# An attention and feed-forward kernel on one core: every queue in the order of a list schedule, one whole pair a block

## The chip, the core and the metric

The kernel runs on one core of a Trainium2 chip. The core has a matrix engine (PE, or TensorE, with its weight loads shown as PEld), three engines for elementwise work (DVE or VectorE, ACT or ScalarE, POOL or GpSimd), a queue that issues transfers (SP), and sixteen DMA engines behind it. Each engine takes its instructions in the order of its own queue; between engines, an instruction waits on semaphores. The metric is the time of one execution in microseconds of device time. Lower is better.

## What is computed

Four batches of 12480 tokens with 128 features go through an induced-attention step with 32 inducing rows, and the result through a feed-forward layer with 2048 hidden values. The weights come as 64-bit numbers.

```python
def mab(q, kv):
    s = scale * (q @ kv.transpose(0, 2, 1))
    s = s - s.max(-1, keepdims=True)
    a = np.exp(s)
    a /= a.sum(-1, keepdims=True) + 1e-09
    return a @ kv
h = mab(I, x)                 # 32 rows over all tokens of the batch
x = mab(x, h)                 # every token over the 32 rows
h = x @ w_in                  # 128 -> 2048
g = np.where(h > 0.0, h, np.exp(np.minimum(h, 0.0)) - 1.0)
return (g @ w_out).astype(np.float32)
```

## The kernel before

**Tiling.** A batch is 25 blocks, 15 of 512 tokens and 10 of 480, in seven groups (`GROUPING`). Hidden values are handled in eight pairs of two chunks of 128 each, so a block has eight pairs and the kernel has 800. Pair number n is (batch x 25 + block) x 8 + pair; `ph_253` is the layer-one result of pair 253.

**A pair.** `ffn_in`: two matmuls into `ph` (three buffers in the accumulation memory, PSUM), then `e = exp(ph - 1)` on ACT. The first product is folded: instead of the token's attention output, the layer takes its 32 attention weights (`stk`, stacked in a high part twice and a low part) against `hw`, the attended rows already multiplied by `w_in`, with a row of ones that adds 1. `ffn_mid`: DVE takes `min(max(ph, 1), e)`, which is the wanted activation plus 1. `ffn_split` makes it ready for layer two in one of three ways, set by `PLAN`:

- "N", whole: POOL subtracts 1 from `e`, and layer two multiplies it in full fp32.
- "P": ACT makes a high part `gh`, POOL subtracts 1 from `e` and then makes the low part `gl = e - gh`.
- "D": ACT makes `gh`, and DVE makes `gl`; the pair keeps its `ph` until then.

`ffn_out` adds the pair into `po`, one bank of PSUM per block: for a split pair six matmuls in a single-pass format (`gh` with the high and the low part of the weight, `gl` with the high part, for two chunks), for a whole pair two matmuls in fp32. `PLAN` is "PDNPDPND": three P, three D and two N a block. After the eighth pair DVE transposes `po` into `o`, and four transfers store it.

**The rest.** For every batch there is a first half: load and transpose the tokens (`load_xT`, line 239), scores against the inducing rows, a maximum per phase (two phases of groups), exponentials, and `gather`, the product with the tokens (`ps_hh`), then the normalised rows `hn`, `hT4`, and `hw`. The second half (`attend_...`) takes the scores of each token against the 32 rows, with a softmax over them whose subtraction, multiplication and low part (`alo`) are on POOL, and places the result in `stk` by transfers. The first half of batch b+1 runs beside the feed-forward work of batch b. The first batch has nothing to run beside: `first_batch` loads the tokens, takes the 64-bit weights apart with integer and float steps on DVE, ACT and POOL (`Weight`), and makes the first block's `stk` on DVE alone (line 526). The loads of `w_out` go into buffers that hold tokens before.

**The order.** PE runs in the order in which the program is written: layer one of pair n, layer two of the pair five behind, and then the middle steps of pair n-1; attention steps are put between by a table of due times in blocks (`attend`, `first_half`). The other engines' queues are ordered by the language's scheduler, but for a few instructions that keep the program's order (the `xT` transposes and the exponentials of the first half). Buffers: five `e`, four `gh`, three `gl`, six `s`.

## Time and profile before

| | us |
|---|---|
| median of three runs | 1728.04 (1726.66 to 1728.49) |
| span of the profiled execution | 1726.8 |
| PE busy | 1655.4 (96%) |
| DVE busy | 1532.5 (89%) |
| ACT busy | 1404.8 (81%) |
| POOL busy | 1347.0 (78%) |

The profile gives no time of the profiled execution other than its span; it lies within the three runs. Busy time of PE is not work at its peak: a matmul's shown duration covers its way through the array, and the next one starts before it ends (a 480-token matmul is shown with 0.38 us, and the next one starts 0.22 us later). So prices of PE work are taken from start to start. The same holds in small for DVE and ACT, whose shown durations overlap by about 0.1 us.

### The profile page before, as it was taken

What the parts mean: (1) busy time and instruction counts of PE and PEld (TensorE: products, weight loads), DVE (VectorE), ACT (ScalarE), POOL (GpSimd) and SP (SyncE); (2) the same over time, 40 slices, a digit from 0 to 9 for tenths busy, and PEclk for the clock granted to TensorE, in tenths of its full rate; (3) what the DMA queues carried; (4) which work ended last, traced back from release to release, by engine and by line L of the source; (5) the groups of instructions that cost most, each with busy time, mean ns of one, the idle gap of its engine ahead of it and who ended that gap; (6) DMA issues with size and microseconds to landing.
All of it is one profiled execution on the core that took longest, in us unless ns stands there. A gap on an engine that the chain in (4) does not pass through costs nothing.

```text
span 1726.8 us, 22653 instructions
## 1 busy us (share of the span) xinstructions
PE 1655.4 (96%) x7446; PEld 1174.4 (68%) x7446; DVE 1532.5 (89%) x1618; ACT 1404.8 (81%) x1643; POOL 1347.0 (78%) x970
## 2 busy tenths in 40 slices
PE   6689999999999999999999999999999999999998
PEld 4356766677676666667776676676777777777776
DVE  6889889989899989898899989889989999989986
ACT  6778888788788878878888788788878888888886
POOL 3877778778787877777778777777868888888886
PEclk9599999999999999999999999999999999999999
DMA  7363233322234333232323423412212211121111
GB/s 253 62 95 54 58 64 59 64 50 61 58 52 74 54 75 60 48 61 45 84 50 54 73 61 50 79 35 36 72 30 48 37 32 27 23 37 31 26 19 21
DMA packets 384757, 98.12 MB, mean 57 GB/s; under 512 B 364864, under 2 KB 370784, under 8 KB 384384
## 3 DMA queue, kind: packets, MB, share of 16 engines
q1 hardware_dynamic: 384640, 96.68, 29.0%
q8 instruction: 59, 0.97, 0.2%
q14 instruction: 58, 0.48, 0.1%
HBM read 48.94 MB, written 25.56 MB: 43 GB/s over the span
## 4 chain that ended last, share of the span: by engine, by line
PE 78%; DVE 9%; ACT 4%; issue 3%; DMA 2%; POOL 2%; SPq 0%; DVEq 0%; ACTq 0%; POOLq 0%
PE po L616 56%; PE ph L558 19%; DVE e L572 2%; ACT e L566 2%; DVE xT L239 2%; DVE gl L584 2%; DVE ph L572 1%; PE ps_hh L367 1%; ACT gh L581 1%; PE ps_t L483 1%; PE ps_s L291 1%; DMA w_raw<-in_moe_w_in_dram 1%; DMA xm<-in_x_dram 1%; DMA xq<-in_x_dram 1%; DVE o L623 1%
## 5 line engine op out<-in xcount | busy, mean ns | idle before, releaser
L566 ACT ACTIVATE e<-ph 128x1024 f32<-128x1024 f32 (+1 forms) x800 | 804.0, 1006 | 235.3 <-PE ph L558 228.3
L589 POOL TENSOR_SCALAR e<-e 128x1024 f32<-128x1024 f32 (+1 forms) x500 | 512.3, 1031 | 307.6 <-ACT gh L581 261.7
L594 POOL TENSOR_TENSOR gl<-e,gh 128x1024 fp32r<-128x1024 f32 (+1 forms) x300 | 704.1, 2347 | 17.6
L572 DVE SCALAR_TENSOR_TENSOR e<-ph,e 128x1024 f32<-128x1024 f32 (+1 forms) x500 | 592.2, 1188 | 78.5 <-ACT e L566 76.4
L558 PE MATMUL ph<-stk,hw 128*128 128x512 f32 (+1 forms) x1600 | 566.0, 435 | 33.1 <-DVE gl L584 14.9
L616 PE MATMUL po<-gh,wo_h 128*128 128x512 f32 (+1 forms) x1200 | 469.1, 391 | 10.5 <-ACT e L566 6.5
L616 PE MATMUL po<-gh,wo_l 128*128 128x512 f32 (+1 forms) x1200 | 465.7, 388 | 0.0
L558 PEld LDWEIGHTS ph<-stk,hw 128*128 128x128 f32 x1600 | 293.5, 190 | 211.4 <-issue 100.6
L572 DVE SCALAR_TENSOR_TENSOR ph<-ph,e 128x1024 f32<-128x1024 f32 (+1 forms) x300 | 359.2, 1197 | 45.2 <-ACT e L566 44.0
L584 DVE SCALAR_TENSOR_TENSOR gl<-ph,gh 128x1024 fp32r<-128x1024 f32 (+1 forms) x300 | 355.9, 1186 | 26.5 <-ACT e L566 10.1
L616 PE MATMUL po<-gl,wo_h 128*128 128x512 f32 (+1 forms) x1200 | 368.5, 388 | 2.4 <-POOL gl L594 2.4
L616 PE MATMUL po<-e,wo_n 128*128 128x512 f32 (+1 forms) x800 | 367.2, 581 | 0.0
L581 ACT ACTIVATE gh<-e 128x1024 fp32r<-128x1024 f32 (+1 forms) x300 | 311.4, 1038 | 21.9 <-DVE e L572 17.8
L581 ACT ACTIVATE gh<-ph 128x1024 fp32r<-128x1024 f32 (+1 forms) x300 | 301.0, 1003 | 10.2 <-DVE ph L572 8.6
L616 PEld LDWEIGHTS po<-gh,wo_h 128*128 128x128 f32 x1200 | 226.0, 188 | 63.3 <-ACT s L300 5.6
L616 PEld LDWEIGHTS po<-gl,wo_h 128*128 128x128 f32 x1200 | 225.8, 188 | 47.7 <-POOL gl L594 3.5
L616 PEld LDWEIGHTS po<-gh,wo_l 128*128 128x128 f32 x1200 | 226.3, 189 | 45.5 <-issue 0.4
L616 PEld LDWEIGHTS po<-e,wo_n 128*128 128x128 f32 x800 | 151.0, 189 | 106.2 <-issue 91.7
L623 DVE STREAM_TRANSPOSE o<-po 128x512 f32<-128x512 f32 (+1 forms) x100 | 69.3, 693 | 12.1 <-PE po L616 12.1
L239 DVE STREAM_TRANSPOSE xT<-xq 128x1024 f32<-128x1024 f32 (+2 forms) x39 | 45.2, 1160 | 0.0
L367 PE MATMUL ps_hh<-xm,e 128*32 128x128 f32 (+2 forms) x872 | 33.3, 295 | 8.2 <-DVE bias L324 2.4
L500 POOL TENSOR_TENSOR s<-s,mx 128x512 f32<-128x512 f32 (+3 forms) x28 | 28.8, 1027 | 14.7 <-DVE mx L499 14.6
(94 smaller groups left out, 575.1 us busy)
## 6 DMA issues: line engine op xcount, KB each, us to landing
xm<-in_x_dram SPq DMA_DIRECT2D x32, 512.0 KB, 4.5
out_dram<-o SPq DMA_DIRECT2D x240, 64.0 KB, 2.0
xq<-in_x_dram SPq DMA_DIRECT2D x84, 128.0 KB, 3.6
out_dram<-o SPq DMA_DIRECT2D x160, 60.0 KB, 1.9
stk<-ahi SPq DMA_DIRECT2D x118, 64.0 KB, 2.0
xq<-in_x_dram SPq DMA_DIRECT2D x60, 120.0 KB, 3.4
stk<-ahi SPq DMA_DIRECT2D x80, 60.0 KB, 2.0
stk<-alo SPq DMA_DIRECT2D x59, 64.0 KB, 2.0
```

The source lines that it names most:

```text
L239: tc.keep_in_program_order(nc.vector.transpose(t, xq.rearrange("p u d -> p (u d)")))
L367: nc.tensor.matmul(ps[c * Q : (c + 1) * Q, :C], st["e", g][:np_, u * Q : (u + 1) * Q], st["xm", g, u - u % UP][:np_, u % UP, :], start=(u ...
L500: eng.tensor_tensor(out=s, in0=s, in1=mx.unsqueeze(2).broadcast_to([np_, U, Q]), op=ALU.subtract)
L558: nc.tensor.matmul(ph[:, i], state[b]["hw"][:, f * P : (f + 1) * P], stacks[b, k], start=True, stop=True,)
L566: nc.scalar.activation(e, ph, AF.Exp, bias=-1.0)
L572: nc.vector.scalar_tensor_tensor(out=v["g"], in0=v["ph"], scalar=1.0, in1=v["e"], op0=ALU.max, op1=ALU.min)
L581: nc.scalar.activation(v["gh"], v["g"], AF.Copy, bias=-1.0)
L584: nc.vector.scalar_tensor_tensor(out=v["gl"], in0=v["g"], scalar=-1.0, in1=v["gh"].bitcast(F32), op0=ALU.add, op1=ALU.subtract,)
L589: nc.gpsimd.tensor_scalar(out=v["e"], in0=v["e"], scalar1=-1.0, scalar2=1.0, op0=ALU.add, op1=ALU.mult)
L594: nc.gpsimd.tensor_sub(v["gl"], v["e"], v["gh"].bitcast(F32))
L616: nc.tensor.matmul(po[:, :T], w, g, start=(cp == 0 and i == 0), stop=(cp == NCP - 1 and i == len(parts) - 1),)
L623: nc.vector.transpose(o.rearrange("p u d -> p (u d)"), po[:, :T])
```

## The change

**A list schedule.** The kernel no longer writes its instructions down as it goes. Each one is recorded as an `Op` with its engine, a key (where it is wanted, in pairs), a length and a delay worked out by small formulas, and what it reads and writes. `Program.order()` then goes through all of them, with buffers, PSUM banks and transfers kept account of: at each step it takes, over the engines, the ready instruction that can start first (for ACT and DVE the one of smallest key among those that could start within 60 ns). The instructions are issued in the order of the starts so found, and `manual_schedule()` without a list of engines keeps that order on every queue, SP's included.

**The plan** is "PDPDPDPN": four P, three D, one N.

**Layer two** is recorded in two pieces for a split pair (`gh` and `gl`); the first piece issued for a block starts the sum, the last one ends it, whichever they are.

**The first batch** runs its maxima in five phases of groups instead of two, so that first gathers do not wait for later groups; the weights are taken apart in slices of 512 instead of 256, with the sign put in by integer operations on DVE (one ACT and one POOL instruction less a slice); `hn` is made on ACT.

**Buffers**: `gl` has two for P and two for D pairs, `s` five instead of six. The step that adds 1e-9 to a row sum (line 511) is a two-input form with a tile of zeros.

```diff
-PLAN = "PDNPDPND"
+PLAN = "PDPDPDPN"
+KMID, KGL, KOUT = 1.0, 1.6, 5.0
+KGH = {"D": 1.5, "P": 2.0}
+BUF = dict(e=5, gh=4, glD=2, glP=2)
+LOOKS = {"PE": 0.0, "ACT": 60.0, "DVE": 60.0, "POOL": 0.0, "SP": 0.0}
...
+    def order(self):
...
+        while len(done) < len(self.ops):
+            best = None
+            for e, row in there.items():
...
+                for op in row:
+                    if op.at is not None and op.at <= base + self.LOOK[e]:
+                        if cand is None or (op.key, op.n) < (cand.key, cand.n):
+                            cand = op
+                if best is None or cand.at < best.at:
+                    best = cand
...
+        return sorted(done, key=lambda o: (o.start, o.n))
+
+def act(n, psum=False):
+    return 0.828 * n + (54 if psum else 69), 118.0
...
+        add("DVE", key + 4.0, dve(n, True)[0], lambda: nc.vector.transpose(
+            t(), xq().rearrange("p u d -> p (u d)")
+        ), r=[(xq, dq) for dq in range(4)], w=[(t, 0)], lag=108)
...
+        add("DVE", n + KMID, dve(2 * T)[0], lambda: nc.vector.scalar_tensor_tensor(
+            out=ga(), in0=ph()[:, :, :T], scalar=1.0, in1=e(), op0=ALU.max, op1=ALU.min
+        ), r=[(ph, 0), (e, 0)], w=[(g, 0)], lag=108)
...
+        pieces = [[v for v in parts if v[0] < 2], [v for v in parts if v[0] == 2]]
+        for m, piece in enumerate(pieces):
...
+            def layer_two(piece=piece):
+                for _, w, g_ in piece:
+                    nc.tensor.matmul(
+                        po()[:, :T], w(), g_(), start=po.count == 0, stop=po.count == po.total - 1
+                    )
+                    po.count += 1
...
-        nc.vector.tensor_scalar_add(sm, sm, EPS)
+        add("DVE", later, 62.0, lambda: nc.vector.scalar_tensor_tensor(
+            out=sm()[:np_], in0=sm()[:np_], scalar=EPS, in1=none[:np_, :U],
+            op0=ALU.add, op1=ALU.add,
+        ), r=[(sm, 0)], w=[(sm, 0)], lag=108)
...
-    PHASES = [range(0, 3), range(3, NG)]
+    PHASES0 = [range(0, 2), range(2, 4), range(4, 5), range(5, 6), range(6, 7)]
+    PHASES = [range(0, 3), range(3, NG)]
...
-    ctx.enter_context(tc.issue_after(last.ins))
-    ET = mybir.EngineType
-    ctx.enter_context(tc.manual_schedule(engines={ET.PE}))
+    todo = prog.order()
+    ctx.enter_context(tc.manual_schedule())
+    for op in todo:
+        op.fn()
```

**Three places where the order changes.** The first is PE in the seventh block of batch one. `ph` is layer one, `po` layer two; the first number after `ph`, `gh`, `gl` or `e` is that of the pair. Before:

```order
L558 MATMUL ph_254_5545<-stk1_135,hw_1_4194 128x512 x2
L616 MATMUL po_1_6_5533<-gh_249_5473,wo_h_127 128x512
L616 MATMUL po_1_6_5533<-gh_249_5473,wo_l_128 128x512
L616 MATMUL po_1_6_5533<-gh_249_5473,wo_h_127 128x512
L616 MATMUL po_1_6_5533<-gh_249_5473,wo_l_128 128x512
L616 MATMUL po_1_6_5533<-gl_249_5475,wo_h_127 128x512 x2
L558 MATMUL ph_255_5562<-stk1_135,hw_1_4194 128x512 x2
L616 MATMUL po_1_6_5533<-e_250_5464,wo_n_126 128x512 x2
L558 MATMUL ph_256_5571<-stk2_137,hw_1_4194 128x512 x2
```

The same place of the changed kernel:

```order
L736 MATMUL ph_254_5879<-stk1_177,hw_1_498 128x512 x2
L736 MATMUL ph_255_5882<-stk1_177,hw_1_498 128x512 x2
L796 MATMUL po_1_6_5826<-gl_250_5870,wo_h_174 128x512 x2
L796 MATMUL po_1_6_5826<-gl_251_5868,wo_h_174 128x512 x2
L796 MATMUL po_1_6_5826<-gh_252_5872,wo_h_174 128x512
L796 MATMUL po_1_6_5826<-gh_252_5872,wo_l_175 128x512
L796 MATMUL po_1_6_5826<-gh_252_5872,wo_h_174 128x512
L796 MATMUL po_1_6_5826<-gh_252_5872,wo_l_175 128x512
L796 MATMUL po_1_6_5826<-gh_253_5885,wo_h_174 128x512
L796 MATMUL po_1_6_5826<-gh_253_5885,wo_l_175 128x512
L796 MATMUL po_1_6_5826<-gh_253_5885,wo_h_174 128x512
L796 MATMUL po_1_6_5826<-gh_253_5885,wo_l_175 128x512
```

Before, every layer one was followed by the whole of the pair five behind. Now two layer ones stand in a row (in this block 251 and 253 are D pairs, 250, 252 and 254 are P, 255 is the N pair), `gh` and `gl` pieces of different pairs follow, and layer two is two to four pairs behind.

The second is POOL beside it. `L589` and `L765` subtract 1 from `e`; `L594` and `L769` make `gl`; the row with `s2` is a step of the attention's softmax. Before:

```order
L589 TENSOR_SCALAR e_248_5413<-e_248_5413 128x1024
L594 TENSOR_TENSOR gl_248_5441<-e_248_5413,gh_248_5438 128x1024
L589 TENSOR_SCALAR e_250_5464<-e_250_5464 128x1024
L589 TENSOR_SCALAR e_251_5480<-e_251_5480 128x1024
L594 TENSOR_TENSOR gl_251_5526<-e_251_5480,gh_251_5523 128x1024
L589 TENSOR_SCALAR e_253_5531<-e_253_5531 128x1024
L589 TENSOR_SCALAR e_254_5548<-e_254_5548 128x1024
L594 TENSOR_TENSOR gl_253_5560<-e_253_5531,gh_253_5557 128x1024
```

Now:

```order
L765 TENSOR_SCALAR e_248_5784<-e_248_5784 128x1024
L769 TENSOR_TENSOR gl_248_5833<-e_248_5784,gh_248_5810 128x1024
L765 TENSOR_SCALAR e_250_5804<-e_250_5804 128x1024
L769 TENSOR_TENSOR gl_250_5870<-e_250_5804,gh_250_5831 128x1024
L765 TENSOR_SCALAR e_252_5847<-e_252_5847 128x1024
L769 TENSOR_TENSOR gl_252_5899<-e_252_5847,gh_252_5872 128x1024
L765 TENSOR_SCALAR e_254_5895<-e_254_5895 128x1024
L765 TENSOR_SCALAR e_255_5905<-e_255_5905 128x1024
L769 TENSOR_TENSOR gl_254_5947<-e_254_5895,gh_254_5916 128x1024
```

Four subtractions in eight pairs stand where three stood, each right behind the step that it needs.

The third is PE in the first batch, before any feed-forward work: `ps_x` transposes tokens, `ps_s` are scores of a group (the number behind it), `ps_pm` is part of a maximum, `ps_hh` gathers a group. Before:

```order
L291 MATMUL ps_s_4_381<-xT_8_358,indT 32x480 x2
L291 MATMUL ps_s_4_381<-xT_9_359,indT 32x480 x2
L291 MATMUL ps_s_5_423<-xT_10_400,indT 32x480 x2
L259 MATMUL ps_x_8_453<-ident,xm_6_8_177 128x64 x7
L291 MATMUL ps_s_5_423<-xT_11_401,indT 32x480 x2
L291 MATMUL ps_s_6_462<-xT_12_442,indT 32x480 x2
L367 MATMUL ps_hh_0_482<-xm_0_0_151,e_0_480 32x128 x8
```

Now:

```order
L477 MATMUL ps_pm_0_344<-apart_0_329,nsel_160 128x8
L866 MATMUL ps_x_0_348<-ident,xm_3_0_213 128x96 x8
L451 MATMUL ps_s_2_360<-xT_4_340,indT 32x512 x2
L451 MATMUL ps_s_2_360<-xT_5_342,indT 32x512 x2
L523 MATMUL ps_hh_0_374<-xm_0_0_197,eT_0_366 32x128 x8
L523 MATMUL ps_hh_0_374<-xm_0_8_201,eT_0_366 32x128 x8
L523 MATMUL ps_hh_1_396<-xm_1_0_205,eT_1_372 32x128 x8
L523 MATMUL ps_hh_1_396<-xm_1_8_207,eT_1_372 32x128 x8
L866 MATMUL ps_x_8_430<-ident,xm_3_8_218 128x96 x8
```

The first gather, behind which the buffers of two token pieces come free for the loads of `w_out`, stood behind the scores of all seven groups and now stands behind those of three.

More of the change, by code (lines that the diff above doesn't have):

```diff
@@ L219 @@
-    xT = {}
-    state = {}
-    steady = []
-    def in_order(ins):
-        return tc.keep_in_program_order(ins) if steady else ins
-    def load_xT(b, h):
+    ind = const.tile([M, C], F32, name="ind")
+    indT = const.tile([C, M], F32, name="indT")
+    win_sb = const.tile([C, F], F32, name="win_sb")
+    wo_n = const.tile([P, max(1, len(CHUNKS_N)), C], F32, name="wo_n")
+    wo_h = const.tile([P, NSPLIT, C], F32R, name="wo_h")
+    wo_l = const.tile([P, NSPLIT, C], F32R, name="wo_l")
+    homes = [const.tile([P, TM], F32R, name=f"stk{i}") for i in range(STK)]
@@ new lines, in block_xT, with parts_xT, start @@
+    def block_xT(b, k):
+        h, j = HALF_OF[k]
+        T = BLOCKS[k][1]
+        return xT[b, h]()[:, j * T : (j + 1) * T]
+    def parts_xT(b, k):
+        h, _ = HALF_OF[k]
+        U = BLOCKS[k][1] // Q
+        return [(xT[b, h], v) for v in range(0, 1 if b else U, UP)]
+    def start(b, key):
+        st = get(b)
+        st["pm"] = new([P, NG], F32, "pm", f"pm_{b}")
+        st["es"] = new([P, NG], F32, "es", f"es_{b}")
+        add("POOL", key, 60.0, lambda: nc.gpsimd.memset(st["pm"](), -3.0e38),
+            w=[(st["pm"], g) for g in range(NG)], lag=45)
+        add("POOL", key, 60.0, lambda: nc.gpsimd.memset(st["es"](), 0.0),
+            w=[(st["es"], g) for g in range(NG)], lag=45)
@@ new lines @@
+    for i, groups in enumerate(PHASES0):
+        for g in groups:
+            transpose_first(g)
+            scores(0, g, CH + g)
+        bias_of(0, i, groups.stop, CH + groups.stop - 1)
+        for g in groups:
+            weights_of(0, g, i, CH + g)
+            gather(0, g, CH + g, g == 0, get(0)["scale", i] if i and g == groups.start else None)
+    sum_es(0, PHASES0, CH + 7)
+    share_of(0, CH + 7)
+    norm_h(0, CH + 7)
+    spread_h(0, CH + 7)
+    attend(0, 0, CH + 8, 0.0, lone=True)
@@ new lines, with piece @@
+    project_h(0, CH + 8)
+    for quarter in range(4):
+        n = NFC // 4
+        raw = new([P, n, 2 * C], U32, "xm" if quarter < 2 else "e", f"w_out_{quarter}")
+        rows = w_out[quarter * n * P : (quarter + 1) * n * P, :]
+        load_raw(raw, lambda raw=raw, rows=rows: nc.sync.dma_start(
+            raw(), rows.rearrange("(c p) d -> p c d", p=P)), LOADS[3] + 0.01 * quarter)
+        prog.writer[("w_out",)] = prog.ops[-1]
+        key = KWOUT + quarter * KWSTEP
+        done = (raw, 0, "lo")
+        weight_steps(raw, 0, key, lambda raw=raw: words_of(raw, 0)[0].bitcast(F32), [done])
+        for j in range(n):
+            f = quarter * n + j
+            def piece(raw=raw, j=j):
+                return words_of(raw, 0)[0].bitcast(F32)[:, j * C : (j + 1) * C]
+            if f in WHERE_N:
+                add("ACT", key + 0.1 * j, act(C)[0], lambda f=f, piece=piece: nc.scalar.copy(
+                    wo_n[:, WHERE_N[f], :], piece()), r=[done], w=[("wo", f)], lag=118)
@@ L641, in first_half, with key @@
+                add("POOL", key + 0.1 * j, pool_two(C)[0] + 100,
+                    lambda w=w, piece=piece: nc.gpsimd.tensor_sub(
+                        wo_l[:, w, :], piece(), wo_h[:, w, :].bitcast(F32)
+                    ), r=[done, ("woh", f)], w=[("wo", f)], lag=50)
     def first_half(b):
-        steps = [(0.0, lambda: start(b))]
+        base = (b - 1) * NBLK
+        def key(at):
+            return (base + at) * NCP
+        start(b, key(0.0))
         at = 0.0
+        first = 0.0
@@ L665, in first_half @@
+                gather(b, g, key(at + 1.19), g == 0,
+                       get(b)["scale", i] if i and g == PHASES[i].start else None)
                 at += gap
[L666 to L672 removed]
```

1193 lines of the change are left out of this document (646 added, 547 removed).

## The prediction

> **What bounds the kernel now.** I read the page's first part, then the busy time in four stretches of the same phase of the work, then the chain of waits inside a stretch, then single rows.
>
> ```profile
> span 1726.8 us, 22653 instructions
> PE 1655.4 (96%) x7446; PEld 1174.4 (68%) x7446; DVE 1532.5 (89%) x1618; ACT 1404.8 (81%) x1643; POOL 1347.0 (78%) x970
> ```
>
> The span stands 1.2 us under the median of the runs (1728.04); the sum is made against the span and the forecast is given as it comes out. The page shows nothing around the span that would add to it.
>
> ```profile
> core 0: us, PE busy (x) PEld busy (x) DVE busy (x) ACT busy (x) POOL busy (x), PEclk, DMA share, GB/s
> 89.13:507.79 418.66, 406.52 (x1825) 287.26 (x1826) 375.77 (x386) 341.37 (x386) 324.78 (x223) 1.00 0.33 61
> 507.79:926.47 418.68, 408.64 (x1836) 287.50 (x1835) 377.15 (x389) 342.94 (x388) 326.37 (x223) 1.00 0.32 60
> ...
> 1344.82:1726.80 381.98, 376.72 (x1514) 277.10 (x1513) 336.79 (x328) 317.36 (x351) 313.53 (x214) 1.00 0.16 28
> ```
>
> Each stretch is one batch of 25 blocks (the cuts are at the same layer-two pair of each batch's first block; the third of the four, left out, ends 418.4 us after its start, at 1344.82). PE is busy for 408.6 of 418.7 us and idle for 10; in the last batch, where no next batch's first attention half runs beside it, it is idle for 5.3 us of 382.0, and that lies at the end:
>
> ```profile
> by line: PE po L616 74.2%; PE ph L558 23.0%; PE ps_t L483 1.5%; DVE o L623 0.2%; issue 0.0%
> ...
> 1721.58 0.68 DVE L623 STREAM_TRANSPOSE o<-po 128x480 f32<-128x480 f32 x1 [3.91 <-PE po L616]
> ```
>
> The first row is the chain of waits in the last batch: nothing but matmuls. PE's work is the bound there to the last 5 us, which are the transpose from 1721.58 and the store behind it. In batch one the chain holds other things:
>
> ```profile
> by line: PE po L616 54.3%; PE ph L558 18.5%; issue 3.6%; DVE e L572 3.3%; DVE xT L239 2.9%; DVE gl L584 2.7%; ACT e L566 2.7%; ACT gh L581 1.8%; PE ps_hh L367 1.7%; DVE ph L572 1.5%; PE ps_s L291 1.4%; DMA xq<-in_x_dram 1.4%; PE ps_t L483 1
> ...
> 533.36 3.40 DMA xq<-in_x_dram
> 563.63 2.31 DMA xq<-in_x_dram
> ```
>
> These are places where DVE's queue stood at a transpose whose load had not landed, and PE then lacked a `ph` buffer. So PE's work sets the pace, and order costs some 10 us a batch.
>
> **The whole pair that becomes a split one.** PE first. A whole (N) pair is four passes of fp32 matmul, a split pair six single ones:
>
> ```profile
> 1353.72 1.72 PE po L616 x4
> ...
> 1662.43 1.61 PE po L616 x4
> 1664.48 1.31 PE po L616 x6
> ```
> ```profile
> 1355.73 0.39 PE L616 MATMUL po<-gh,wo_h 128*128 128x512 f32 x1
> ...
> 1357.11 0.63 PE L558 MATMUL ph<-stk,hw 128*128 128x512 f32 x2
> ```
>
> The first fence is the chain (1.72 us for an N pair of 512 tokens, 1.61 at 480, a split pair 1.31 at 480); in the second, a split pair of 512 lasts from 1355.73 to 1357.11, 1.38. A batch has 15 blocks of 512 and 10 of 480, so PE loses 15 x 0.34 + 10 x 0.30 = **8.1 us a batch**: 408.6 becomes 400.5, and the last batch's 376.7 becomes 368.6.
>
> ACT gains one `gh` a block, POOL one subtraction (the pair's `-1` on POOL stays, since an N pair had it too):
>
> ```profile
> L594 POOL TENSOR_TENSOR gl<-e,gh 128x1024 fp32r<-128x1024 f32 (+1 forms) x76 | 178.4, 2347 | 4.7
> L581 ACT ACTIVATE gh<-e 128x1024 fp32r<-128x1024 f32 (+1 forms) x76 | 78.9, 1038 | 6.0 <-DVE e L572 4.7 <-PE ps_t L483 0.4 <-PE ps_hh L367 0.4
> ...
> L531 POOL TENSOR_TENSOR alo<-aT,ahi 128x512 fp32r<-128x512 f32 (+3 forms) x7 | 8.8, 1258 | 0.0
> L513 POOL TENSOR_TENSOR s<-s,sm 128x512 f32<-128x512 f32 (+3 forms) x7 | 7.3, 1036 | 0.0
> L500 POOL TENSOR_TENSOR s<-s,mx 128x512 f32<-128x512 f32 (+3 forms) x7 | 7.2, 1027 | 3.7 <-DVE mx L499 3.7
> L511 DVE TENSOR_SCALAR sm<-sm 128x16 f32<-128x16 f32 (+3 forms) x7 | 2.9, 420 | 0.0
> ```
>
> These groups are of batch one. ACT: 342.9 + 25 x 1.04 = 369 us a batch. DVE keeps 377, less about 2 for the EPS step of line 511, which becomes another form; both stay under PE's 400. POOL is the question, and its busy time alone misleads, since a subtraction waits for the `-1` just ahead of it:
>
> ```profile
> 1430.49 1.06 POOL L589 TENSOR_SCALAR e<-e 128x1024 f32<-128x1024 f32 x1 [1.41 <-ACT gh L581]
> 1431.63 2.39 POOL L594 TENSOR_TENSOR gl<-e,gh 128x1024 fp32r<-128x1024 f32 x1
> 1433.97 1.07 POOL L589 TENSOR_SCALAR e<-e 128x1024 f32<-128x1024 f32 x1
> ...
> 1704.45 1.00 POOL L589 TENSOR_SCALAR e<-e 128x960 f32<-128x960 f32 x1 [1.30 <-ACT gh L581]
> 1705.53 2.24 POOL L594 TENSOR_TENSOR gl<-e,gh 128x960 fp32r<-128x960 f32 x1
> 1707.74 0.99 POOL L589 TENSOR_SCALAR e<-e 128x960 f32<-128x960 f32 x1
> ```
>
> From start to start a P pair holds POOL for 1.14 + 2.34 = 3.48 us at 512 and 1.08 + 2.21 = 3.29 at 480. With four of them and one lone `-1` (1.0) a block takes 14.9 and 14.1: 15 x 14.9 + 10 x 14.1 = 365 a batch, and with the attention's three groups (23) and one memset of about 1.8 it is **POOL 389 us a batch against PE's 400**, 97%. In the last batch three of the groups' first steps lie ahead of it in the new order, so POOL has 380 and PE 368.6. There POOL becomes the bound: 380 + 5.2 for the end is 385 against 382.0 now, **+3 us**. Bounds: 374 if POOL's lead hides it all (-8), 397 if POOL stands idle for 3% (+15).
>
> A rule speaks against the added subtraction. The Trainium skill, "GPSIMD Engine Reference", section 4.1 "Engine selection", says to put elementwise work on the Vector engine, where two-input operations take about half the time. The row of line 594 (2347 ns) beside DVE's `gl` below (1186 ns) agrees with the factor. By that rule the new pair would be of kind D, and DVE would carry 25 x 1.1 = 28 us more a batch, 405 in all, past PE's 400: here POOL is the place with room, and the sum is left as it is.
>
> ```profile
> L584 DVE SCALAR_TENSOR_TENSOR gl<-ph,gh 128x1024 fp32r<-128x1024 f32 (+1 forms) x76 | 90.2, 1186 | 8.3 <-ACT e L566 3.4 <-PE po L616 3.2 <-ACT gh L581 0.8
> ```
>
> **The order.** In the new one the `xT` transposes stand four pairs (some 7 us) behind their loads, so the two DMA waits above go; the scores, gathers and `alo` are spread between pairs; layer one comes as two pairs in a row with both D and P parts summed when they are there. What is late next: a `ph` buffer of a D pair, freed only by its second DVE step, and `gl`, with two buffers for P and two for D instead of three for all. Walking pairs 248 to 257 in the new order (a part of it stands above), PE has about 8 us of work between `ph_253` and `ph_256`, and the D pair's path (exp 1.0, DVE 1.2, `gh` 1.0, DVE 1.2, hand-overs) about 5: it fits, with 3 us for what else ACT and DVE hold. Summing in any order is worth little by itself, as PE's wait for POOL's `gl` is 5.9 us in the whole run (3.5 for the weight load, 2.4 for the matmul). I bound PE's idle time per batch by 0 (its middle of the last batch, with the others at 82 to 88%) and by 25 (two and a half times today's 10, for POOL at 97%) and take **6**, between the row of the last batch and today's, since the waits on loads go and POOL's come. A batch is then 400.5 + 6 = 406.5 against 418.6: **-12 us, three times -36** (bounds -54 and +21).
>
> **The start.**
>
> ```profile
> 32.95 3.04 SPq L200 DMA_DIRECT2D w_raw<-in_moe_w_out_dram  x4
> 52.71 0.86 DVE L409 TENSOR_SCALAR hn<-h,r 128x128 f32<-128x128 f32 x1
> 67.00 1.11 DVE L526 TENSOR_TENSOR stk<-aT_-1_804,stk 32x512 fp32r<-32x512 f32 x1
> 68.16 1.22 PE L558 MATMUL ph<-stk,hw 128*128 128x512 f32 x2 [9.36 <-DVE stk L526]
> 77.94 0.88 POOL L214 TENSOR_TENSOR wo_l<-wo,wo_h 128x128 fp32r<-128x128 f32 x2
> 83.92 1.88 PE L616 MATMUL po<-e,wo_n 128*128 128x512 f32 x4
> ...
> 40.00:60.00 20.00, 12.64 (x136) 7.63 (x136) 15.50 (x36) 14.65 (x41) 14.75 (x25) 0.50 0.58 95
> 70.00:85.00 15.00, 11.99 (x33) 7.76 (x28) 12.31 (x14) 11.69 (x17) 13.51 (x14) 0.66 0.00 0
> ```
>
> The loads of `w_out` wait for a buffer until the first gather is done, at 32.95; the first layer one starts at 68.16, and the weights are being finished until 78. In the new order the first two gathers stand ahead of groups 3 to 6, so `w_out` can be asked for about 8 us sooner; its words stand ahead of the last groups on DVE and ACT, so `hn` gains 5 or 6 us and not 8; from `hn` to layer one (14.6 us now, with 4 us of weight steps in between) 1 us goes. First layer one at about 61, **-7**. From 68.16 to the N pair at 83.92 pass 15.8 us with 7 us of full-speed PE work in them; with all weights done before, I take another **-6**. Together **-13**, bounds -5 (the weights only change places) and -20. PE runs at half clock there (0.50 and 0.66 granted in the last two rows), which stays.
>
> **Sum.** 1726.8 - 13 - 36 + 3 = 1681.
>
> **Rivals.** *The order takes nearly every wait*: PE idle 1 a batch, batches of 401.5 (-51), start -20, end +3: 1659. For it: the last batch runs without any. Against: POOL at 97% where it was 78%. *Most is given back*: idle 15 a batch (415.5, -9 in all), start -10, end +6: 1714. For it: ACT, DVE and POOL all stand above 90% of PE's time, in queues that keep their order. *POOL sets the pace, slower than before*: POOL's work is 3 x 389 + 380 = 1547, and what lies around the four batches in the forecast is 1681 - 3 x 406.5 - 385 = 76. Before each of its 400 subtractions POOL has to see `gh` of ACT and a `gl` buffer read by PE.
>
> ```profile
> POOL e L589 <- ACT gh L581: 261.7, 217, 4.4
> ```
>
> Such waits are 1.2 us each today and cost nothing while POOL has room. Where they cost over (1727 - 76 - 1547) / 400 = 0.26 us a subtraction, the kernel is slower; at 0.3 us it takes 1743. Against: a look-ahead of several pairs in the rows, and `gh` stands two or more rows ahead on ACT. *POOL's subtraction stretches as DVE gets denser*: at 5% (a size I choose, since no row shows one) it is 400 x 0.12 = 47 us on POOL, so 401 a batch, level with PE, and 392 in the last: 12 us more there make 1693. The trace shows none of it: 2347 ns in batch one, and the row below in the last.
>
> ```profile
> L594 POOL TENSOR_TENSOR gl<-e,gh 128x1024 fp32r<-128x1024 f32 (+1 forms) x74 | 173.9, 2350 | 3.8
> ```
>
> The Trainium skill, "GPSIMD Engine Reference", section 1 "Specifications", names this one: the memory ports are shared with the Vector engine, in contention when its instruction has two SBUF inputs. Here nearly all of DVE's steps read one side from PSUM.
>
> **How the numbers follow.** Forecast 1681: 0.45. Nearly no wait, 1659: 0.20. Given back, 1714: 0.18. Stretched, 1693: 0.04. POOL's pace, 1743: 0.13. The forecast's own range is 1665 to 1698. The range of 1650 to 1726 leaves out the slower case and the tip of the fastest, under 2 in 10. 0.2% of the time is 3.5 us, about what a measurement of this kernel can tell from none. Slower by more: 0.13; within: 0.04, the upper end of the given-back case; faster: 0.83.
>
> **What would show it.** Right: PE busy near 400 in a full batch and idle under 10; POOL busy near 385; in the last batch PE waiting for POOL's `gl`, and that line in the chain; first layer one near 61. Wrong: POOL idle between pairs for `gh` while PE waits for `gl` (the slower case); PE idle above 15 with `ph` waiting for DVE (given back); a first layer one at 66 or later; a subtraction above 2.45 us.

## The result, and the profile after

The changed kernel takes **1746.47 us** (median of 4 runs, 1744.96 to 1747.35) against 1727.94 of the kernel before beside it: ratio **1.0109, 95% interval 1.0094 to 1.0123**. It is slower, and outside the range of 1650 to 1726 that was given.

The first two lines of the page after stand beside those of before: PE 12 us more, ACT 83 and POOL 217 more.

```profile
span 1744.0 us, 23334 instructions
...
PE 1667.7 (96%) x7652; PEld 1198.6 (69%) x7652; DVE 1530.7 (88%) x1610; ACT 1487.9 (85%) x1710; POOL 1564.5 (90%) x1041
```

To compare stretches, the prediction's cut (the first block's whole pair) no longer serves: that pair was the third of eight and is now the last. The cut used from here on is the start of DVE's transpose of `po`, the end of a block, for the first block of each batch and for the last block of all. Both views are of busy time in stretches: from, to, length, then each engine's busy time and number of instructions, and behind POOL the granted clock. First the kernel before:

```profile
0.00:101.89 101.89, 66.48 (x481) 42.28 (x482) 75.27 (x137) 68.94 (x142) 64.90 (x96) 0.78 0.57 149
101.89:523.10 421.21, 410.53 (x1847) 290.11 (x1847) 381.04 (x394) 344.67 (x391) 329.63 (x227) 1.00 0.32 60
523.10:941.77 418.67, 408.63 (x1836) 287.48 (x1835) 377.17 (x389) 342.99 (x388) 326.37 (x223) 1.00 0.32 60
941.77:1358.19 416.42, 406.43 (x1827) 286.19 (x1826) 374.41 (x386) 341.71 (x387) 322.88 (x221) 1.00 0.28 52
1358.19:1721.58 363.39, 363.35 (x1461) 268.38 (x1459) 323.87 (x316) 306.44 (x339) 303.23 (x206) 1.00 0.17 29
```

The changed kernel:

```profile
0.00:119.18 119.18, 74.37 (x506) 44.78 (x506) 81.82 (x139) 61.46 (x109) 57.17 (x69) 0.76 0.58 147
119.18:533.94 414.76, 408.54 (x1904) 294.66 (x1904) 377.79 (x395) 366.72 (x417) 385.63 (x252) 1.00 0.29 61
533.94:953.14 419.20, 409.70 (x1884) 293.33 (x1884) 380.55 (x395) 365.46 (x415) 383.84 (x249) 1.00 0.31 62
953.14:1364.04 410.90, 404.88 (x1863) 294.56 (x1864) 367.36 (x379) 361.69 (x410) 381.19 (x247) 1.00 0.22 47
1364.04:1738.90 374.86, 370.24 (x1497) 271.25 (x1495) 322.47 (x308) 332.56 (x363) 356.64 (x228) 1.00 0.14 26
```

So of the 17.2 us between the two spans, the start has **+17.3**, the three batches **-11.4** (-6.5, +0.5, -5.5), the last stretch **+11.5**, and the end behind it -0.1. The forecast for the same three terms was -13, -36 and +3 (at cuts some 13 us earlier). The four stretches behind the start sum to the same as before, and what the kernel loses is the start.

The chain of waits of the last stretch, by line, was all matmuls before (quoted in the prediction). After, an eighth of it is POOL:

```profile
by line: PE po L796 50.7%; PE ph L736 16.9%; POOL gl L769 7.3%; ACT e L746 4.3%; issue 4.1%; POOL e L765 4.0%; ACT gh L755 3.2%; DVE gl L760 2.2%; DVE e L750 1.8%; DVE ph L750 0.9%; POOL alo L705 0.8%; DMA stk<-ahi 0.7%; POOLq L1012 0.6%; D
```

The start, rows of the timeline by engine (start, length; in brackets the idle time before and what ended it):

```profile
23.72 2.39 SPq L901 DMA_DIRECT2D w_out<-in_moe_w_out_dram  x4
...
27.97 0.77 DVE L364 TENSOR_SCALAR w_part<-w_in 128x512 uint32<-128x512 uint32 x2 [2.62 <-DMA w_in<-in_moe_w_in_dram]
31.77 0.69 DVE L378 SCALAR_TENSOR_TENSOR w_part<-w_in,w_part 128x512 uint32<-128x512 uint32 x1 [2.83 <-POOL w_part L374]
35.45 1.28 DVE L875 COPY xT<-ps_x 128x512 f32<-128x512 f32 x2
...
36.19 1.93 PE L451 MATMUL ps_s<-xT,indT 128*32 128x512 f32 x6 [8.18 <-DVE xT L875]
83.45 2.92 PE L736 MATMUL ph<-stk,hw 128*128 128x512 f32 x6
```

DVE waits for the load of `w_in` and then for POOL at its weight slices, with copies of tokens queued behind them until 35.45; PE stands 8.18 us for one of these copies, and the first layer one comes at 83.45 instead of 68.16. The delay is there before the attended rows are normalised: the step `hn` starts at 68.62, where before it started at 52.71. The loads of `w_out` are asked for 9 us sooner, as foreseen.

### The profile page after: what moved, and what is told of

It is laid out like the page before. It is cut to its first block, busy times and chain, and to the rows that moved or that the text cites. A ratio compares the mean times of both kernels' runs of the same rounds, so it can differ in the third digit from the quotient of the medians.

```text
span 1744.0 us, 23334 instructions
## 1 busy us (share of the span) xinstructions
PE 1667.7 (96%) x7652; PEld 1198.6 (69%) x7652; DVE 1530.7 (88%) x1610; ACT 1487.9 (85%) x1710; POOL 1564.5 (90%) x1041
## 4 chain that ended last, share of the span: by engine, by line
PE 63%; POOL 13%; DVE 11%; issue 6%; ACT 5%; DMA 2%; SPq 0%; POOLq 0%; DVEq 0%; ACTq 0%
PE po L796 45%; PE ph L736 15%; POOL gl L769 7%; POOL e L765 4%; DVE e L750 3%; ACT e L746 2%; DVE gl L760 2%; DVE ph L750 2%; ACT gh L755 2%; PE ps_t_False L645 1%; PE ps_s L451 1%; POOL alo L705 1%; PE ps_hh L523 1%; DVE apart L471 1%; DVE sm_False L679 1%
## 5 line engine op out<-in xcount | busy, mean ns | idle before, releaser
L769 POOL TENSOR_TENSOR gl<-e,gh 128x1024 fp32r<-128x1024 f32 (+1 forms) x400 | 940.0, 2351 | 19.5
L765 POOL TENSOR_SCALAR e<-e 128x1024 f32<-128x1024 f32 (+1 forms) x500 | 511.9, 1031 | 100.2 <-ACT gh L755 87.0
L796 PE MATMUL po<-gh,wo_h 128*128 128x512 f32 (+1 forms) x1400 | 557.1, 398 | 3.7 <-DVE o L807 2.0
L796 PE MATMUL po<-gh,wo_l 128*128 128x512 f32 (+1 forms) x1400 | 546.1, 390 | 0.0
L736 PE MATMUL ph<-stk,hw 128*128 128x512 f32 (+1 forms) x1600 | 488.9, 405 | 25.2 <-DVE e L750 16.3
L755 ACT ACTIVATE gh<-e 128x1024 fp32r<-128x1024 f32 (+1 forms) x400 | 417.9, 1045 | 39.1 <-DVE e L750 35.9
L796 PE MATMUL po<-gl,wo_h 128*128 128x512 f32 (+1 forms) x1400 | 444.0, 410 | 5.9 <-POOL gl L769 5.6
L796 PEld LDWEIGHTS po<-gl,wo_h 128*128 128x128 f32 x1400 | 253.4, 188 | 118.4 <-POOL gl L769 55.3
L796 PEld LDWEIGHTS po<-gh,wo_h 128*128 128x128 f32 x1400 | 263.7, 188 | 85.8 <-ACT gh L755 14.7
L796 PEld LDWEIGHTS po<-gh,wo_l 128*128 128x128 f32 x1400 | 263.6, 188 | 54.1 <-issue 3.3
L796 PE MATMUL po<-e,wo_n 128*128 128x512 f32 (+1 forms) x400 | 187.5, 591 | 0.5 <-POOL e L765 0.5
L796 PEld LDWEIGHTS po<-e,wo_n 128*128 128x128 f32 x400 | 75.7, 192 | 58.6 <-issue 48.6
L807 DVE STREAM_TRANSPOSE o<-po 128x512 f32<-128x512 f32 (+1 forms) x100 | 69.2, 692 | 11.5 <-PE po L796 11.2
L451 PE MATMUL ps_s<-xT,indT 128*32 128x512 f32 (+1 forms) x200 | 33.0, 642 | 16.8 <-DVE xT L875 10.7
```

The lines of the kernel that those rows point to most:

```text
L451: nc.tensor.matmul(ps()[j * Q : (j + 1) * Q, :T], indT, block_xT(b, g0 + j), start=True, stop=True)
L736: nc.tensor.matmul(ph()[:, j, :T], st["hw"]()[:, f * P : (f + 1) * P], homes[i][:, :T], start=True, stop=True,)
L755: add("ACT", n + KGH[how], act(2 * T, how == "D")[0], lambda: nc.scalar.activation(gh(), ga(), AF.Copy, bias=-1.0), r=[(g, 0)], w=[(gh, 0) ...
L765: add("POOL", n + KMID, pool_one(2 * T)[0], lambda: nc.gpsimd.tensor_scalar(out=e(), in0=e(), scalar1=-1.0, scalar2=1.0, op0=ALU.add, op1= ...
L769: add("POOL", n + KMID, pool_two(2 * T)[0], lambda: nc.gpsimd.tensor_sub(gl(), e(), gh().bitcast(F32)), r=[(e, 0), (gh, 0)], w=[(gl, 0)], ...
L796: nc.tensor.matmul(po()[:, :T], w(), g_(), start=po.count == 0, stop=po.count == po.total - 1)
```

## The experiments

All twelve runs, cut as above (us; the last column is the measured ratio to the kernel before with its interval):

| | to the first block's end | batch | batch | batch | last | median | ratio |
|---|---|---|---|---|---|---|---|
| before | 101.9 | 421.2 | 418.7 | 416.4 | 363.4 | 1728 | |
| after | 119.2 | 414.8 | 419.2 | 410.9 | 374.9 | 1746.5 | 1.0109 [1.0094, 1.0123] |
| e1 after, WARM 0 | 104.7 | 414.6 | 419.2 | 410.9 | 374.8 | 1735.4 | 1.0035 [1.0024, 1.0047] |
| e2 after, old plan | 119.7 | 420.4 | 419.9 | 411.6 | 378.9 | 1758.4 | 1.0174 [1.0159, 1.0189] |
| e3 before, new plan | 98.5 | 426.6 | 423.2 | 421.8 | 372.2 | 1750.0 | 1.0127 [1.0110, 1.0144] |
| e4 after, one piece | 121.2 | 426.1 | 424.1 | 418.9 | 377.5 | 1774.2 | 1.0266 [1.0251, 1.0281] |
| e5 after, light POOL | 117.1 | 409.1 | 408.5 | 400.8 | 365.5 | 1708.1 | 0.9892 [0.9875, 0.9908] |
| e6 after, no tiny steps | 119.1 | 411.4 | 410.9 | 407.1 | 376.0 | 1731.0 | 1.0016 [1.0007, 1.0025] |
| e7 e1 + true durations | 103.8 | 412.7 | 415.8 | 411.9 | 379.4 | 1730.6 | 1.0016 [1.0007, 1.0025] |
| e8 e3, light POOL | 101.3 | 418.1 | 416.5 | 415.5 | 366.8 | 1725.3 | 0.9986 [0.9976, 0.9995] |
| e9 e1 + e6 | 103.6 | 411.4 | 410.6 | 407.3 | 375.8 | 1714.7 | 0.9924 [0.9912, 0.9937] |
| e10 before, no tiny steps | 101.5 | 421.3 | 417.8 | 415.4 | 364.1 | 1727.1 | 0.9998 [0.9989, 1.0006] |
| e11 e9, later hand-over | 102.6 | 412.7 | 411.1 | 407.8 | 368.5 | 1711.3 | 0.9905 [0.9890, 0.9920] |
| e12 e11, old plan | 104.9 | 411.7 | 408.2 | 405.4 | 379.9 | 1717.0 | 0.9936 [0.9920, 0.9953] |

**e1: the schedule's PE lengths at the start.** The schedule counts every PE length twice before `WARM` (in `order()`: `if op.eng == "PE" and start < self.warm: hold *= 2`).

```diff
-WARM = 40000.0
+WARM = 0.0
```

> The changed kernel, but its schedule is made as if PE ran at full clock from the start (WARM 0 instead of 40000 ns). Theory start-order (the schedule held PE's steps at double length before 40 us, where the trace grants full clock, so token copies and gathers were queued on DVE and ACT behind weight steps): the first layer one moves from 83 us to 68 to 74, the total falls by 9 to 16 us against the changed kernel (1746), to about 1733. Rival start-work (five phases and weights done early are simply more work ahead of the first layer one): first layer one stays at 80 or later, total within 4 us of 1746.

1735.4 us, 11 less than the changed kernel by the medians and 14.7 less by the spans of the profiled executions (1729.3 and 1744.0); that of e1 is the fastest of its six, and where the others lose up to 5 us is not shown. The cut shows where: the first block ends at 104.7 instead of 119.2 (-14.5), and nothing else moves by more than 0.2. In its trace `hn` starts at 51.84 and the first layer one comes at 71.86:

```profile
71.86 2.50 PE L736 MATMUL ph<-stk,hw 128*128 128x512 f32 x5
```

For the doubling there is no ground in the trace: in the first 40 us the granted clock was 0.99 before, and 0.90 even in the changed kernel with its stalls. With PE thought slow, the schedule set DVE's weight slices ahead of the token copies for which PE then stood; in e1 the first slice of `w_in` starts on DVE at 30.13, behind most of these copies.

**e2 and e3: the plan and the order apart.** e2 is the changed kernel with the old plan, e3 the kernel before with the new one.

```diff
-PLAN = "PDPDPDPN"
+PLAN = "PDNPDPND"
```

> The changed kernel with the plan of before (two whole pairs a block). Theory POOL-bound: the last batch, 383 us of which POOL was busy 360 and PE waited for its low parts, falls to 380 at the same cut less about 8, the three other batches come to 410 to 413 from 415 on the mean, the total falls to 1722 to 1732, with the start as late as in the changed kernel. Rival list-order: the order itself costs PE its time, so that with PE's work up by 8 us a batch the batches take 420 or more and the total is 1755 or more.

> The kernel before, with the plan of the changed one and nothing else. Theory POOL-bound: start as before (first layer one at 68), the last batch 390 to 395 (10 above before) and the three others within 6 us of before, total 1725 to 1740. Rival list-order (POOL is no bound, the new order spoils it): batches 8 us shorter each and the last one as well, total near 1697.

Neither part pays alone. e2 lands in the range of its second theory, 1755 or more. e3 lies above both: its batches and its last stretch are as its first theory had them, its total is 10 us over. The new plan in the old order costs 22 us, though it takes PE work away: the batches are 4.5 to 5.4 longer, the last stretch 8.8. In that run PE waits for DVE's `gl` ahead of layer one. The D pairs, three a block as before, now stand at every second place, and each keeps its `ph`; that this is the reason was not tried alone:

```profile
PEld ph L558 <- DVE gl L584: 87.5, 88, 2.2
...
PE ph L558 <- DVE gl L584: 37.4, 48, 1.8
```

(us in all, times, longest; the same two rows before are 24.8 and 14.9.) The old plan in the new order speaks against the view that POOL's load alone makes the changed kernel slow: with POOL at 325 to 328 a batch two of the three batches stay where they were before (the third is 4.8 shorter), and the last stretch is 15.5 longer. With about the same load on POOL as before, PE's weight loads wait for its `gl` ten times as long (the first row is of the kernel before, the second of e2), so the new order alone sets layer two close behind POOL:

```profile
PEld po L616 <- POOL gl L594: 3.5, 3, 2.8
```
```profile
PEld po L796 <- POOL gl L769: 37.0, 89, 0.9
```

**e4: layer two in one piece again.** A split pair's six matmuls are issued together, after both `gh` and `gl`.

```diff
-        pieces = [[v for v in parts if v[0] < 2], [v for v in parts if v[0] == 2]]
+        pieces = [parts]
...
-            reads = [(e, 0)] if how == "N" else [(gh, 0)] if m == 0 else [(gl, 0)]
+            reads = [(e, 0)] if how == "N" else [(gh, 0), (gl, 0)]
```

> The changed kernel with layer two of a split pair recorded in one piece, which waits for both parts. If summing in any order is what keeps PE fed: 5 to 20 us slower than the changed kernel (1751 to 1766), with more PE waiting for POOL's low part. If it is worth little: within 4 us of 1746.

It is 27.7 us slower than the changed kernel (11.4, 4.9 and 8.0 in the batches, 2.6 in the last stretch, 2.0 at the start): more than expected. Two pieces are worth much in this order, where POOL's part comes late. The schedule is made anew from the joined pieces, so the other queues change with them.

**e5 and e8: POOL made light.** Its subtraction reads one input, in the changed kernel and in e3.

```diff
-            add("POOL", n + KMID, pool_two(2 * T)[0], lambda: nc.gpsimd.tensor_sub(
-                gl(), e(), gh().bitcast(F32)
-            ), r=[(e, 0), (gh, 0)], w=[(gl, 0)], lag=50)
+            add("POOL", n + KMID, pool_two(2 * T)[0], lambda: nc.gpsimd.tensor_scalar(
+                out=gl(), in0=gh().bitcast(F32), scalar1=-1.0, scalar2=1.0, op0=ALU.add, op1=ALU.mult
+            ), r=[(e, 0), (gh, 0)], w=[(gl, 0)], lag=50)
```

> The changed kernel with the subtraction of the low part on POOL (L769, two inputs, 2351 ns) turned into an operation with one input (gh alone, about 1.03 us): the low part of those pairs is left out of the result, the order of every queue stays. POOL's work falls by about 100 x 1.3 = 130 us a batch, from 386 to some 255. If POOL running near full is what makes PE wait since the change, the batches (from the end of one batch's first block to the end of the next one's) fall from 414.8, 419.2, 410.9 to 401-407 each, the last stretch from 374.9 to 357-364, and the whole to 1696-1715. If the order itself costs the time and POOL is only where it shows, the batches stay at 409-418 and the whole at 1735-1748. The start stays near 119 under both.

> The kernel before with the new plan (one whole pair a block) and POOL's subtraction turned into a one-input operation, as in the run on the changed kernel; the low part of those pairs is left out. With the subtraction this order took 426.6, 423.2, 421.8 a batch against 421.2, 418.7, 416.4 with two whole pairs, though PE has 8 us less to do. If POOL's load is what took the 8 us and 5 more, the batches fall to 405-413 and the whole to 1695-1715. If the plan loses for another reason (which engine a pair's parts stand on in the queues), they stay at 418-427 and the whole at 1738-1752.

The step goes from 2351 to 1031 ns, and the same order of the same instructions runs 38 us faster (5.7, 10.7, 10.1 in the batches, 9.4 in the last stretch). Two of the batches stayed a little over the 401 to 407 expected, and the last stretch over its 357 to 364. PE's waits for POOL's `gl` are gone from the view, and the chain of its last stretch has 1.4% of POOL:

```profile
by line: PE po L796 62.2%; PE ph L736 20.2%; ACT e L746 3.5%; ACT gh L755 3.4%; issue 2.0%; DVE gl L760 1.8%; POOL e L765 1.4%; DVE e L750 1.3%; PE ps_t_False L645 0.8%; DMA stk<-alo 0.5%; DMA stk<-ahi 0.5%; ACTq L1012 0.3%; POOL alo L705 0
```

In the old order (e8), with PE's queue as in e3 and small differences on DVE and ACT, the same edit gives 24.7 us back. It lands between the two expectations: the batches come out 1 to 3 us under before, not 8. Of the 39.6 us by which e3's three batches miss the plan's 8.1 each, 21.5 come back. So POOL's load is a large part there, and not all of it: PE's waits for DVE's `gl` shown for e3 stay in part, with 60.7 and 22.1 us. Made light, POOL has 250 us a batch, less than the 326 of the kernel before, so this is more than a return to its old load would give.

**e6 and e10: tiny VectorE steps that wait for POOL.** In the changed kernel one row of `apart`, 28 columns, is shown with 3.95 us. The timeline around it, DVE, POOL and PE:

```profile
709.99 1.40 DVE L679 SCALAR_TENSOR_TENSOR sm_False<-sm_False,none 64x15 f32<-64x15 f32 x1
...
715.60 3.95 DVE L471 TENSOR_TENSOR apart<-pm,mine 128x28 f32<-128x28 f32 x1
719.48 1.21 DVE L750 SCALAR_TENSOR_TENSOR e<-ph,e 128x1024 f32<-128x1024 f32 x1
...
710.34 1.04 POOL L765 TENSOR_SCALAR e<-e 128x1024 f32<-128x1024 f32 x1
...
715.14 2.06 POOL L765 TENSOR_SCALAR e<-e 128x1024 f32<-128x1024 f32 x2
717.17 2.33 POOL L769 TENSOR_TENSOR gl<-e,gh 128x1024 fp32r<-128x1024 f32 x1
721.87 1.04 POOL L765 TENSOR_SCALAR e<-e 128x1024 f32<-128x1024 f32 x1 [2.36 <-ACT gh L755]
...
720.74 0.73 PE L736 MATMUL ph<-stk,hw 128*128 128x512 f32 x2 [3.55 <-DVE e L750]
```

The addition of 1e-9 from 709.99 ends at 711.39, POOL's operation beside it at 711.38. `apart` stands until 719.55 (715.60 + 3.95), and POOL's third operation in a row ends at 719.50; then POOL has nothing to do, and DVE goes on. PE stands 3.55 us behind it. The groups of the two kinds, `apart` and the addition of 1e-9 (shortest, median, longest in ns), before and after:

```profile
L316 DVE TENSOR_TENSOR apart<-pm,mine x8: 135/665/966, 23.0 to 1191.7; 128x12 f32<-128x12 f32 x4, 128x28 f32<-128x28 f32 x4
L511 DVE TENSOR_SCALAR sm<-sm x28: 130/318/1030, 79.3 to 1626.6; 128x16 f32<-128x16 f32 x11, 128x15 f32<-128x15 f32 x8, 96x16 f32<-96x16 f32 x5, 64x15 f32<-64x15 f32 x4
```
```profile
L471 DVE TENSOR_TENSOR apart<-pm,mine x11: 158/443/3957, 19.5 to 1132.6; 128x28 f32<-128x28 f32 x4, 128x12 f32<-128x12 f32 x3, 128x8 f32<-128x8 f32 x1, 128x16 f32<-128x16 f32 x1
L679 DVE SCALAR_TENSOR_TENSOR sm_False<-sm_False,none x28: 162/388/2279, 94.7 to 1496.8; 128x16 f32<-128x16 f32 x11, 128x15 f32<-128x15 f32 x8, 96x16 f32<-96x16 f32 x5, 64x15 f32<-64x15 f32 x4
```

Both edits, in the changed kernel (e6) and, in its own words, in the kernel before (e10):

```diff
-        add("DVE", later, 62.0, lambda: nc.vector.scalar_tensor_tensor(
-            out=sm()[:np_], in0=sm()[:np_], scalar=EPS, in1=none[:np_, :U],
-            op0=ALU.add, op1=ALU.add,
-        ), r=[(sm, 0)], w=[(sm, 0)], lag=108)
...
-        add("DVE", key, 4 * n + 60.0, lambda: nc.vector.tensor_tensor(
-            out=apart()[:, :, :n],
-            in0=st["pm"]()[:, :n].unsqueeze(1).broadcast_to([P, 4, n]),
-            in1=mine.unsqueeze(2).broadcast_to([P, 4, n]),
-            op=ALU.mult,
-        ), r=[(st["pm"], g) for g in range(n)], w=[(apart, 0)], lag=108)
+        for c in range(4):
+            add("ACT", key, 75.0, lambda c=c: nc.scalar.activation(
+                apart()[:, c, :n], st["pm"]()[:, :n], AF.Copy, scale=mine[:, c : c + 1]
+            ), r=[(st["pm"], g) for g in range(n)], w=[(apart, c)], lag=118)
```

> The changed kernel without two kinds of tiny VectorE operation whose both inputs lie in SBUF: the addition of 1e-9 to the softmax sums (L679) is left out, and the four products of apart (L471) are made on ScalarE. In the changed kernel one L471 took 3.95 us and one L679 2.28 us where the median is 0.44 and 0.39, and each ended with a POOL operation; together they took 23 us above their shortest. If VectorE stands still for POOL there and PE behind it, the second batch (419.2, with the 3.95) falls by 4-9 us, the whole by 10-22, to 1724-1737. If the time is absorbed elsewhere, the whole stays at 1741-1748.

> The kernel before with the same two edits (line 511's addition of 1e-9 left out, apart on ScalarE). There POOL is busy 78% and the two kinds took 12 us above their shortest (1.03 the longest), against 23 in the changed kernel (3.95 the longest). If it is POOL's long unbroken runs that make these operations costly, this kernel gains 0 to 4 us: 1724-1729. If the edits gain by themselves, whatever POOL does, it gains as much as the changed kernel did, 10-16: 1712-1719.

e6 gains 15.5 us, 3.4, 8.3 and 3.8 in the batches, as the first theory had it, and nothing in the last stretch. Above the shortest of their shape the two kinds of step take 4.9, 6.9 and 6.7 us in the changed kernel's batches. The second and the third batch hold one stop of 3.95 us each (the other is at 1132.59), and PE stands idle for 3.55 us behind both. The rest of the gain is not tied to single stops: e6's schedule is made anew without these steps, and in e7 below a schedule made anew moved single batches by up to 3.4 us. e10 gains nothing that can be measured. With POOL at 78% the stops are short and hidden; with POOL in long unbroken runs they last for microseconds. e3, the old order with POOL at 383 to 387 us a batch, shows this without the new order:

```profile
L316 DVE TENSOR_TENSOR apart<-pm,mine x8: 135/1074/2186, 23.3 to 1199.7; 128x12 f32<-128x12 f32 x4, 128x28 f32<-128x28 f32 x4
L511 DVE TENSOR_SCALAR sm<-sm x28: 133/366/2159, 80.3 to 1646.6; 128x16 f32<-128x16 f32 x11, 128x15 f32<-128x15 f32 x8, 96x16 f32<-96x16 f32 x5, 64x15 f32<-64x15 f32 x4
```

The 1e-9 step has one input there, and it is stopped all the same. So it is not the new two-input form that lets it be stopped.

**e7: true durations in the schedule.** WARM 0, and the formulas for the lengths raised to the trace's.

```diff
-    return 0.828 * n + (54 if psum else 69), 118.0
+    return 0.828 * n + (54 if psum else 97), 118.0
...
-    return 1.042 * n + (88 if transpose else 45), 108.0
+    return 1.042 * n + (96 if transpose else 64), 108.0
...
-    return passes * n / 2.4 + (17 if passes == 1 else 5), 165.0
+    return passes * n / 2.4 + (20 if passes == 1 else 85), 165.0
```

> The changed kernel with WARM at 0 as before, and with the schedule's durations raised to those of the trace (a 1024-wide VectorE operation 1131 ns, not 1112; a ScalarE one from SBUF 945, not 917; a pass of 512 columns 233, not 230; a whole pair's matmul 80 ns more). If the list order loses its time because each piece is set so closely after its input that small errors in the durations turn into waits, the batches fall from 414.6, 419.2, 410.9 to 403-409 each and the whole to 1705-1722. If the durations matter little, it stays within 5 us of the run with WARM 0 alone (1735): 1730-1740.

1730.6, at the lower end of the second expectation. Two batches are 1.9 and 3.4 shorter than in e1, the third 1.0 and the last stretch 4.6 longer. Wrong durations are not the cause.

**e9 and e11: the two causes together, and a later hand-over.** e9 takes the edits of e1 and e6. e11 also lets the schedule count POOL's result as there 550 ns later, so that PE's pieces that read it stand further back.

```diff
-            ), r=[(e, 0), (gh, 0)], w=[(gl, 0)], lag=50)
+            ), r=[(e, 0), (gh, 0)], w=[(gl, 0)], lag=600)
```

> The changed kernel with WARM at 0 and without the two kinds of tiny VectorE operation (the addition of 1e-9 is left out, apart is made on ScalarE). If the two causes are separate, the start's gain (119.2 to 104.7) and the batches' (414.8, 419.2, 410.9 to 411.4, 410.9, 407.1) add up: first block done near 104.5, the whole at 1746.5 - 11.0 - 15.5 = 1720, in 1717-1723, below the kernel before by 0.3 to 0.6%. If they overlap, 1724-1731.

> As the first of these three, but the schedule counts POOL's subtraction as handed over 550 ns later, so that PE's pieces that read its result are set further back in PE's queue. PE's waits for that result (55 us in the changed kernel, 131 times, 0.42 each) then lie under other matmuls if they are short slips of POOL against the schedule: batches 404-408 and the whole 5-15 below the first kernel of these three, at 1705-1716. If POOL is late because it has no room (93% busy), pieces set later free gl later and POOL waits in turn: within 5 of the first kernel or slower, 1716-1730.

e9 takes 1714.7, under the 1717 to 1723 expected: the two gains add up by the spans (1744.0 - 14.7 - 14.5 = 1714.8; the span of e9 is 1713.7), and the 1720 came from e1's median, which stands 6 us over the span of its fastest run. e11 takes 1711.3, **ratio 0.9905 [0.9890, 0.9920]** to the kernel before: the fastest but for e5, where the low part of the P pairs is left out (e6, e9, e11 and e12 leave out the addition of 1e-9). The waits of PE's weight loads for POOL's `gl`, after, in e9 and in e11:

```profile
PEld po L796 <- POOL gl L769: 55.3, 131, 1.2
```
```profile
PEld po L790 <- POOL gl L763: 58.7, 138, 1.2
```
```profile
PEld po L790 <- POOL gl L763: 18.9, 50, 1.1
```

From e9 to e11 they fall by two thirds, and yet the three batches are 0.6 to 1.3 us longer. All of the gain is in the last stretch (375.8 to 368.5). So each theory holds in a place of its own: at the end the pieces stood too close behind POOL, and in the batches, where POOL has no room, fewer waits for it bring no time.

**e12: the plan once more, with the order mended.** e11 with the old plan.

> As the run with the late hand-over (WARM 0, no tiny VectorE operations, POOL's subtraction counted 550 ns later; 1711.3), but with the old plan of two whole pairs a block: POOL falls from 381 to about 323 a batch, PE's work rises by 8.1. If, once the order is mended, the plan itself pays by PE's work, this run is slower by up to 32 (three batches and the last): 1725-1743. If POOL at 93% had eaten the plan's gain, it comes out level or faster: 1700-1715.

1717.0, just above the second expectation and well under the first. The three batches are 1.0 to 2.9 *shorter* with the old plan, the last stretch 11.4 longer. The 8.1 us of PE work that the plan takes from a batch bring nothing in the batches; in the last stretch, with the order mended, the plan pays more than that.

## Why the prediction was wrong

**The start: -13 given, +17.3 measured.** The step on the loads held (`w_out` at 23.72 against 32.95). What failed is the inference from it: that the weights' steps would slip in ahead and `hn` still gain 5 or 6 us, with layer one near 61. `hn` came 15.9 us later (68.62 against 52.71), and from there to layer one 0.6 of the forecast 1 us went (14.8 against 15.5). The steps of `w_in` stand ahead of the token copies on DVE; their price was never counted. The doubling below `WARM` accounts for 14.5 of the 17.3 (e1). Without it `hn` gains only 0.9, and the first layer one still comes at 71.86, not at 61, 20.0 us behind `hn`. Between `hT` and layer one DVE's attention steps of the first block share the queue with weight slices and token transposes. That reading was not tried alone. The second term, -6 behind the first layer one, did not come either: from there to the first block's end pass 35.7 us, and 32.9 in e1, against 33.7 before. So the start missed by 30 us, the most of the three terms, and some 16 of them have no cause that was tried.

**The plan's PE work: -8.1 a batch given.** The step took for granted that what PE no longer does shortens a batch while PE is the bound. In the old order the batches became longer with the new plan (e3 against before), and with the mended order as well (e11 against e12). In the changed kernel's own order one batch is 5.6 us shorter by it and two are 0.7 shorter (after against e2). Nowhere did a batch give 8.1 while POOL was busy for more than 90% of it. PE's busy time fell by only 2 to 4 us a batch in the first two of these comparisons. What the plan alone is worth with a light POOL was not run.

**PE's idle time: 10 to 6 given.** The view of the batches would have passed this step, as it shows PE idle for 6.2, 9.5 and 6.0 us; but PE was to be busy near 400 and is shown with 408.5, 409.7 and 404.9. The same 1863 matmuls of the third batch are shown with 404.9 us after and 399.1 in e5 (length, then PE's busy time):

```profile
934.62:1335.45 400.83, 399.13 (x1863) 295.92 (x1864) 361.53 (x378) 362.12 (x410) 249.62 (x247) 1.00 0.22 48
```

The order of PE, DVE and ACT is the same in both, so short waits lie inside PE's busy time. On the side of the weight loads, waits for POOL's `gl` are shown with 55.3 us in the run after, and in e5 they are gone. With POOL light the batches sum to 37.9 us less than before ((421.2 - 409.1) + (418.7 - 408.5) + (416.4 - 400.8)), and 36 was forecast. So the forecast of the batches came within 2 us for a kernel whose POOL has much room. That the sizes agree so well is in part luck: PE's busy time fell by 16.7 us in the three batches of e5 and its idle time by 21.2, where 24.3 and 12 were given. POOL's busy time was foreseen rightly (389 given, 381 to 386 measured); what 92 to 93% of a batch costs was not. It gives back 26.5 of the 37.9, and e5, which changes no order, shows that. How the 26.5 divide is argued in part: e6 takes 15.5 away without touching POOL's work, of which 7.1 are PE's idle time behind the two long stops and the rest smaller stops or the order made anew. The other 11 are left for the load itself by subtraction; e5 and e6 were not run together.

**Summing in any order: "worth little by itself".** Wrong: 27.7 us (e4). PE's wait for POOL's `gl` was small in the old order, which set layer two five pairs back (3.5 us for the weight loads), and 37.0 in the new order with the old plan (e2). So it was no measure of what the pieces are worth with layer two close behind POOL.

**The last batch: +3 given, +11.5 measured.** The signs came: POOL stands in the chain, PE waits for its `gl`, and with POOL light it is +2.1. The reason given did not hold. POOL's work was to be the bound with 380 us against PE's 368.6; at the prediction's cut POOL is shown with 370 and PE with 384. With the old plan POOL has 57 us less to do there, and the stretch is 4.0 us longer (e2); e11, with POOL's work unchanged, is 7.4 us shorter than e9. So most of what the last stretch lost were pieces that stood too close behind POOL, not its work. Why PE, with some 8 us less to do there, does not get under 363.4 even in e5 stays open; it does not in the old order either (e8, 366.8).

**The rivals.** "POOL sets the pace" gave 1743, the nearest number, at 0.13. That it came nearest is luck: it took the start at -13 and had the whole loss in the batches, while the start alone makes up for the 17 us that the kernel lost. Its price was not far off. The wait for `gh` fell to 87.0 us in the run from 261.7, 0.22 for each of the 400 subtractions, under the 0.26 from which it was to decide; all of POOL's idle time in the four stretches is 112 us, 0.28 for each. That POOL's load costs PE time holds (e5), by late `gl` and by DVE's stops. "Most is given back" had PE idle for 15 us a batch with the start at -10; shown are 6 to 10 us, and the time lies inside PE's busy time. "POOL's subtraction stretches" fell too: 2351 ns after, 2347 before. The contention was there the other way round: DVE's steps are stretched, not POOL's. The prediction dismissed it because nearly all of DVE's steps read PSUM on one side; the few that don't are tiny, and it is their stops that count.

## What to carry to other kernels

An engine at 93% that feeds the bound engine is not hidden by a lower busy time: lighten it in a trial run, keeping the order, and the difference is its price. Taking work from the bound engine by giving it to a nearly full one can be worth little or nothing (here 8.1 us a batch were forecast), and PE's busy time hides short waits, so compare it between runs of the same matmuls in the same order. In a list schedule, look for constants that contradict the trace (a doubled length at full clock cost 14.5 us), for tiny VectorE steps that read only SBUF beside a busy POOL, and for readers set right behind the engine that has least room.
